# One decode step on one core: D-vectors as rows in four column tiles, FFN columns at stride 3, a row store, and score sums in two halves

## The chip, the cores and the metric

The kernel runs on one core of a Trainium2 chip. The metric is the device time of one execution in microseconds (us), so lower is better. A time called "median" is that of the runs of one kernel in one set of rounds. The "span" of a profile goes from the first to the last instruction and is 1.7 to 2.2 us shorter than the device time of the same execution.

TensorE is written PE (PEld is its weight load), VectorE is DVE, ScalarE is ACT, and SP is the engine that issues most DMAs. LN2 is the second LayerNorm, and `aT` is gelu(gate) times up, the input of down. The "granted clock" is TensorE's, as a share of full speed; the "DMA share" is the mean busy share of the core's 16 DMA engines.

## The reference, cut to what matters

```python
x = A_x                                          # [2, 1, 640], bf16
mod = (silu(c) @ w_mod).reshape(2, 6, 1, -1)     # w_mod [640, 3840]
sa, ca, ga, sb, cb, gb = ...                     # six 640-vectors per row
h = layernorm(x) * (1 + ca) + sa
# attention: 32 heads of 192, the last 1024 of 4096 cached keys
q = h @ wq                                       # wq [640, 6144]
o = softmax(q k^T / sqrt(192)) v
x = x + ga * (o @ wo)                            # wo [6144, 640]
h = layernorm(x) * (1 + cb) + sb
x = x + gb * ((gelu(h @ w_gate) * (h @ w_up)) @ w_down)   # F = 1536
```

There are two batch rows and one query position each. Nearly all the work is reading weights and cache: 76.9 MB.

## The kernel before

Loads are issued in a fixed order from SP: w_mod, then a ring of eight 1.5 MB slots (five of wq, 16 K and 16 V tiles, six of wo), then w_gate, w_up and w_down in three pieces. A slot is loaded again as soon as its reader is done. So the last bytes to arrive are those of w_down, and everything that must be done after their arrival lies bare.

A D-vector (640 numbers per batch row) is kept "transposed": element p*5+j is on partition p. A product that makes such a vector uses the weights as the stationary operand, read with a stride, and two moving columns:

```python
for tl in range(WOT):                     # wo; w_mod and w_down alike
    for j in range(KT):                   # KT = 5: stride 5
        e.matmul(ps[:, BK_M, 2*j:2*j+2], lhsT=wv[:, tl, :, j], rhs=oT[:, t, :], ...)
# gate and up: FC = 12 tiles, so stride 12
lhsT=wv[:, k, :].rearrange("p (m f) -> p m f", f=FC)[:, :, fc]
# ... (cut)
# the score sums of a tile: three pieces of 16, 8 and 8 columns
CHUNKS = [(0, J // 2), (J // 2, J // 4), (3 * J // 4, J // 4)]
# ... (cut)
WD_SPLIT = [(0, 6), (6, 4), (10, 2)]      # w_down's three loads, of 12
# ... (cut)
S.dma("sp", k_dma(out.rearrange("b o (p j) -> p (b o) j", j=KT), finb[:, :, :]), ...)
```

The store at the end therefore writes five neighbouring numbers (10 bytes) per partition and batch row: 256 pieces.

Of the kernel before, what the change touches and what calls it, by code (L numbers as in the profile page):

```python
# [5 lines left out]
ALU = mybir.AluOpType  # L6
# [97 lines left out]
def bass_adaLN_cond__sliding_block_cached__geglu_ffn__decode_kernel(  # L104
# [21 lines left out]
    NQ = H * Dh  # L126
    HQ = 4
# [5 lines left out]
    DD = Dh // NT  # L133
    FC = F // P
    assert B == 2 and D == KT * P and J * PH == W and NQD * HQ == H and NT * P == NQ
    assert DD * NT == Dh and DD * H == P and FC * P == F and J % 8 == 0
    SCALE = float(Dh) ** -0.5
    EPS = 1e-5
    NEG = 1e30
    GC = 512 // J  # L140
    NCH = Dh // GC
    assert GC * NCH == Dh
# [5 lines left out]
    assert SLOT == NQ  # L148
    WOT = 8
    NWO = NT // WOT  # L150
    assert NWO * WOT == NT and WOT * D <= SLOT
    CHUNKS = [(0, J // 2), (J // 2, J // 4), (3 * J // 4, J // 4)]
    WD_SPLIT = [(0, 6), (6, 4), (10, 2)]
    assert FC == 12
    X0 = HQ * DD * (NQD - 1) + DD - 1
    ZW = X0 + DD * (HQ - 1) + P
    QW = 2 * Dh
    NQB = NQ // (HQ * QW)

    es = ExitStack()  # L160
    with es:
# [10 lines left out]
        prod = sb("prod", [P, 2, J, Dh], BF16)  # L172
        qbc = sb("qbc", [P, B, NQD, Dh], BF16)
        qrow = sb("qrow", [P, NQ // HQ], BF16)
# [4 lines left out]
        mask4 = sb("mask4", [P, HQ], F32)  # L179
        mneg = sb("mneg", [P, HQ], BF16)  # L180
        maskc = sb("maskc", [P, P], F32)
        selq = sb("selq", [P, B, P], BF16)
        ztmp = sb("ztmp", [P, 4, 2, HQ], BF16)
        zsel = sb("zsel", [P, 2, ZW], BF16)
        rows = sb("rows", [2 * B, D], BF16)
        scT = sb("scT", [P, KT, B], BF16)
        X2 = sb("X2", [P, 2, KT, B], F32)
        st4 = sb("st4", [P, 4], F32)
        mv = sb("mv", [P, 8], F32)
        rstd = sb("rstd", [P, 2], F32)  # L190
        modT = sb("modT", [P, 6, KT, B], F32)
        opc = sb("opc", [P, 2, KT, B], F32)
        lnt = sb("lnt", [P, 2, KT, B], F32)
# [13 lines left out]
        fin = sb("fin", [P, KT, B], F32)  # L207
        finb = sb("finb", [P, B, KT], BF16)
        ps = es.enter_context(nc.psum_tensor("ps", [P, 8, 512], F32))

        BK_S = (0, 1)
        BK_Q = (2, 3)
# [3 lines left out]
        BK_M = 7  # L216

# [3 lines left out]
        sem_x = S.sem("d_x")  # L221
# [6 lines left out]
        sem_out = S.sem("d_out")  # L228
# [4 lines left out]
        items = [("wq", k) for k in range(KT)] + [("k", 0)]  # L233
        for g in range(1, NG):
            items += [("k", g), ("v", g - 1)]
        items += [("v", NG - 1)] + [("wo", i) for i in range(NWO)]
# [6 lines left out]
        def ring_src(it):  # L243
            kind, i = it
            if kind == "wq":
                return A_wq.rearrange("(p k) n -> p k n", k=KT)[:, i, :], NQ
            if kind == "wo":
                return A_wo.rearrange("(p t) n -> p t n", t=NT)[:, i * WOT:(i + 1) * WOT, :].rearrange("p t n -> p (t n)"), WOT * D
            quad, b = group(i)
            src = A_k_cache if kind == "k" else A_v_cache  # L250
            return src[b, quad * HQ:(quad + 1) * HQ, K0:Sk, :].rearrange("h (p j) d -> p h (j d)", p=PH), SLOT

        def declare_ring(consumed=()):
            ring_state["done"].update(consumed)
            while ring_state["next"] < len(items):
# [8 lines left out]
        S.dma("act", k_dma(rows[0:B, :], c[:, :]), sem_c, writes=["rows"], name="ld_c")  # L264
        S.dma("act", k_dma(rows[B:2 * B, :], A_x.rearrange("b o d -> (b o) d")), sem_x, writes=["rows_x"], name="ld_x")
        wm_dma = S.dma("sp", k_dma(wm_v.rearrange("p k n -> p (k n)"), w_mod.rearrange("(p k) n -> p (k n)", k=KT)), sem_wm,
                       writes=["wm"], name="ld_wm")
        declare_ring()

# [6 lines left out]
             reads=["ident_f"], writes=["ident_b"], name="ident_b")  # L276
        for b in range(B):
# [6 lines left out]
                                                in_=ones_b[:, 0:1].unsqueeze(2).broadcast_to([P, 4, 2 * HQ]),  # L284
                                                pattern=[[-32, 4], [-1, 2 * HQ]],
# [4 lines left out]
        S.op("dve", lambda e: e.memset(ps[:, 0:4, 0:QW], 0.0), writes=[bank(k) for k in range(4)], name="init_Q")  # L290
        S.op("dve", lambda e: e.memset(ps[:, BK_O, 0:ON], 0.0), writes=[bank(BK_O)], name="init_O")
        S.op("dve", lambda e: e.tensor_reduce(out=mask4[:, :], in_=ident_f[:, :].rearrange("p (x h) -> p h x", h=HQ), axis=AX.X, op=ALU.add),
             reads=["ident_f"], writes=["mask4"], name="mask4")

        cx_ps = ps[:, BK_M, 256:256 + 2 * KT].bitcast(BF16).rearrange("p (j r) -> p j r", j=KT)

        def cx_T(e):
            last = None
            for j in range(KT):
                last = e.transpose(cx_ps[:, j, :], rows[:, :].rearrange("r (p j) -> r p j", j=KT)[:, :, j], ident_b[0:2 * B, 0:2 * B])  # L300
            return last
        S.op("pe", cx_T, reads=["rows", "rows_x", "ident_b"], writes=[bank(BK_M)], name="cxT")
        S.op("act", lambda e: e.activation(out=scT[:, :, :], in_=cx_ps[:, :, 0:B], func=ACTF.Silu),
             reads=[bank(BK_M)], writes=["scT"], name="silu")
        S.op("dve", lambda e: e.tensor_copy(out=X2[:, 0, :, :], in_=cx_ps[:, :, B:2 * B]),
             reads=[bank(BK_M)], writes=[("X2", 0)], name="x_f32")

        def ln_norm(tag):
            S.op("dve", lambda e: e.tensor_tensor(out=X2[:, 1, :, :], in0=X2[:, 0, :, :], in1=X2[:, 0, :, :], op=ALU.mult),
                 reads=[("X2", 0)], writes=[("X2", 1)], name=tag + "_sq")  # L310
            S.op("pe", lambda e: e.matmul(ps[:, BK_M, 448:448 + 4 * KT], lhsT=ones_f[:, :],
                                          rhs=X2[:, :, :, :].rearrange("p q j b -> p (q j b)"), start=True, stop=True),
                 reads=[("X2", 0), ("X2", 1), "ones_f"], writes=[bank(BK_M)], name=tag + "_stat")
            S.op("dve", lambda e: e.tensor_reduce(out=st4[:, :].rearrange("p (q b) -> p q b", q=2),
                                                  in_=ps[:, BK_M, 448:448 + 4 * KT].rearrange("p (q j b) -> p q b j", q=2, j=KT),
                                                  axis=AX.X, op=ALU.add),
                 reads=[bank(BK_M)], writes=["st4"], name=tag + "_sum")
            S.op("dve", lambda e: e.tensor_scalar(out=mv[:, 0:4], in0=st4[:, :], scalar1=1.0 / D, scalar2=None, op0=ALU.mult),
                 reads=["st4"], writes=[("mv", 0)], name=tag + "_mean")
            S.op("dve", lambda e: e.tensor_tensor(out=mv[:, 4:6], in0=mv[:, 0:2], in1=mv[:, 0:2], op=ALU.mult),  # L320
                 reads=[("mv", 0)], writes=[("mv", 1)], name=tag + "_msq")
            S.op("dve", lambda e: e.scalar_tensor_tensor(out=mv[:, 6:8], in0=mv[:, 2:4], scalar=EPS, in1=mv[:, 4:6],
                                                         op0=ALU.add, op1=ALU.subtract),
                 reads=[("mv", 0), ("mv", 1)], writes=[("mv", 2)], name=tag + "_var")
            S.op("act", lambda e: e.activation(out=st4[:, 0:2], in_=mv[:, 6:8], func=ACTF.Sqrt),
                 reads=[("mv", 2)], writes=["st4"], name=tag + "_sqrt")
            S.op("dve", lambda e: e.reciprocal(out=rstd[:, :], in_=st4[:, 0:2]),
                 reads=["st4"], writes=["rstd"], name=tag + "_rstd")
            for b in range(B):
                S.op("dve", (lambda b: lambda e: e.tensor_scalar(out=lnt[:, 0, :, b], in0=X2[:, 0, :, b],  # L330
                                                                  scalar1=mv[:, b:b + 1], scalar2=rstd[:, b:b + 1],
                                                                  op0=ALU.subtract, op1=ALU.mult))(b),
                     reads=[("X2", 0), ("mv", 0), "rstd"], writes=[("lnt", 0, b)], name=tag + "_xn%d" % b)

        def ln_mod(tag, opc_idx, s_idx, dst_bf):
            S.op("dve", lambda e: e.tensor_tensor(out=lnt[:, 1, :, :], in0=lnt[:, 0, :, :], in1=opc[:, opc_idx, :, :], op=ALU.mult),
                 reads=[("lnt", 0, 0), ("lnt", 0, 1), ("opc", opc_idx)], writes=[("lnt", 1)], name=tag + "_mulc")
            S.op("dve", lambda e: e.tensor_tensor(out=dst_bf[:, :, :], in0=lnt[:, 1, :, :], in1=modT[:, s_idx, :, :], op=ALU.add),  # L338
                 reads=[("lnt", 1), ("modT", s_idx)], writes=[tag + "_out"], name=tag + "_out")

        ln_norm("ln1")
        S.op("dve", lambda e: e.tensor_scalar(out=mneg[:, :], in0=mask4[:, :], scalar1=-1.0, scalar2=NEG, op0=ALU.add, op1=ALU.mult),
             reads=["mask4"], writes=["mneg"], name="mneg")
# [5 lines left out]
             reads=["ztmp", "zsel"], writes=["zsel"], name="zsel")  # L349

        mod_pe = []

        def mod_part(part, i0, i1):
            def f(e):
                last = None
# [43 lines left out]
        def q_unit():  # L399
            if qstate["n"] >= len(qunits):  # L400
                return
# [268 lines left out]
```

## Time and profile before

| what | value | where it is read |
|---|---|---|
| device time | 195.04 us, median of 3 | times |
| span | 193.1 us | page |
| share of DMA in the chain that ended last | 81% | page, part 4 |
| DMA rate in the loop | 424 to 425 GB/s, share 1.01 | windows |
| PE and DVE in 30 us of the loop | 22 and 20 us busy | windows |
| last piece of w_down has landed | 186.4 us | semaphore events |
| end of down | 188.45 us | timeline |
| store issued, landed | 188.90, 192.7 us | timeline, DMA issues |

Three lines of the page of the kernel before: the busy share of the DMA engines in 40 slices of the span (9 is 90% or more), the bytes they moved, and the queue that fetches instructions (packets, MB, share).

```profile
DMA  7999999999999999999999999999999999999910
GB/s 255 438 392 428 426 428 425 423 428 428 428 421 428 426 425 419 431 417 433 416 433 420 426 422 422 428 422 428 421 425 428 420 415 431 414 435 423 378 71 1
q8 instruction: 13, 0.21, 0.4%
```

The DMA engines are full from the second slice to the 38th. The Trainium skill, "DMA: Bandwidth & Descriptors", Specifications, gives 435 GB/s as the fabric ceiling; the 424 GB/s of the loop agree with it. No reordering of compute inside the loop can speed that up.

The windows view of the kernel before: start and end of the window, its length, then busy time (and instructions) of PE, PEld, DVE, ACT and POOL, then granted PE clock, DMA share and GB/s.

```profile
60.00:90.00 30.00, 22.89 (x279) 17.25 (x278) 20.05 (x35) 5.40 (x15) 0.00 (x0) 0.92 1.01 424
90.00:120.00 30.00, 21.60 (x275) 16.02 (x272) 19.93 (x33) 3.93 (x12) 0.00 (x0) 0.94 1.01 425
182.00:184.00 2.00, 2.00 (x37) 2.00 (x35) 0.00 (x0) 0.00 (x0) 0.00 (x0) 0.50 0.73 297
184.00:186.00 2.00, 1.65 (x30) 1.57 (x29) 0.18 (x1) 0.00 (x0) 0.00 (x0) 0.50 0.29 112
186.00:188.00 2.00, 2.00 (x53) 2.00 (x54) 0.00 (x0) 0.00 (x0) 0.00 (x0) 0.50 0.00 0
```

In the loop, PE and DVE have a quarter to a third of their time free. At the end, the DMA share falls over four microseconds, from 0.73 to nothing: the 16 engines do not finish together.

The end of the timeline of the kernel before: start, duration (both us), engine, line, operation, output and inputs, and in brackets the idle time of the engine just before and what ended it.

```profile
181.80 3.75 PE L587 MATMUL ps<-h2T,r 128*128 128x2 bf16 x60 [0.27 <-DMA r<-in_B_w_up_dram]
185.65 0.18 DVE L598 TENSOR_TENSOR aT<-ps,gl 128x24 bf16<-128x24 f32 x1 [7.94 <-PE ps L587]
185.89 2.56 PE L606 MATMUL ps<-aT,r 128*128 128x2 bf16 x60 [0.35 <-DVE aT L598]
188.49 0.17 DVE L612 TENSOR_TENSOR fin<-ps,modT 128x10 f32<-128x10 f32 x1 [2.65 <-PE ps L606]
188.69 0.18 DVE L615 TENSOR_TENSOR finb<-fin,X 128x10 bf16<-128x10 f32 x1
188.90 0.40 SPq L231 DMA_DIRECT2D out_dram<-finb  x1
```

The up-projection (L587) starts as w_up lands and needs 62.5 ns per matmul. Down (L606) starts when `aT` is ready, not when its weights land. So when the last w_down piece lands at 186.4 us, the kernel is about 2 us behind.

### The profile page before, as it was taken

Reading aid. Unit: us, or ns where it says so; the run is one execution under the profiler, and the core shown is the slowest. Engines: PE = TensorE matmul, PEld = TensorE weight load, DVE = VectorE, ACT = ScalarE, POOL = GpSimd, SP = SyncE. Lnnn points to the kernel's source line nnn. Section 1 sums busy time; section 2 is a strip of 40 time slices with the busy share of each in tenths; the row PEclk is TensorE's granted clock in tenths of the full one; section 3 lists DMA queues with packets and bytes.
Section 4 is the critical chain, followed back from the end, with each engine's and each line's share of the span. In section 5 each row is a group of like instructions: output and inputs, shape, how many; then the busy total and the mean of one; then the engine's idle time right before and its main releaser. Section 6 shows DMA issues by size and latency. Waiting matters only on the chain.

```text
span 193.1 us, 3891 instructions
## 1 busy us (share of the span) xinstructions
PE 124.5 (64%) x1723; PEld 95.2 (49%) x1723; DVE 86.4 (45%) x164; ACT 28.3 (15%) x70; POOL 2.6 (1%) x12
## 2 busy tenths in 40 slices
PE   0108932479768777597597586596595858563990
PEld 0108600158446556475375355384374538463990
DVE  3221000396847747658649549559556600004000
ACT  2300000303211312201101101201111231003000
POOL 5000000000000000000000000000000000000000
PEclk9999999999996999969879999969969975555555
DMA  7999999999999999999999999999999999999910
GB/s 255 438 392 428 426 428 425 423 428 428 428 421 428 426 425 419 431 417 433 416 433 420 426 422 422 428 422 428 421 425 428 420 415 431 414 435 423 378 71 1
DMA packets 7353, 77.13 MB, mean 399 GB/s; under 512 B 1060, under 2 KB 1064, under 8 KB 1448
## 3 DMA queue, kind: packets, MB, share of 16 engines
q1 hardware_dynamic: 7328, 76.88, 94.7%
q8 instruction: 13, 0.21, 0.4%
q14 instruction: 4, 0.03, 0.0%
q10 hardware_dynamic: 8, 0.01, 0.0%
HBM read 76.88 MB, written 0.00 MB: 398 GB/s over the span
## 4 chain that ended last, share of the span: by engine, by line
DMA 81%; DVE 6%; PE 6%; issue 3%; SPq 1%; DVEq 0%
DMA ring<-in_A_k_cache_dram 53%; DMA r<-in_B_w_up_dram 15%; DMA ring<-in_A_wq_dram 13%; DVE prod L419 4%; PE ps L587 2%; PE ps L432 1%; PE ps L606 1%; SPq L231 1%; DVE S_sb L439 1%; PE ps L382 1%; DVE nmx L449 0%; DVE M L442 0%; DVE rden L493 0%; DVE aT L598 0%; DVE finb L615 0%
## 5 line engine op out<-in xcount | busy, mean ns | idle before, releaser
L432 PE MATMUL ps<-prod,ident_b 128*128 128x128 bf16 (+1 forms) x576 | 59.1, 261 | 28.1 <-DVE prod L419 28.0
L419 DVE TENSOR_TENSOR prod<-ring,qbc 128x1536 bf16<-128x1536 bf16 (+1 forms) x48 | 58.1, 1214 | 26.4 <-DMA ring<-in_A_k_cache_dram 26.4
L432 PEld LDWEIGHTS ps<-prod,ident_b 128*128 128x128 bf16 x576 | 45.3, 108 | 42.4 <-DVE prod L419 37.8
L495 ACT ACTIVATE On<-ps,rden 128x384 bf16<-128x384 f32 x16 | 9.3, 580 | 42.8 <-DVE rden L493 39.5
L556 PE MATMUL ps<-oT,ring 128*128 128x2 bf16 x240 | 10.4, 179 | 5.3 <-DMA ring<-in_A_wo_dram 4.9
L484 PE MATMUL ps<-ring,E_sb 128*8 128x384 bf16 x256 | 13.4, 330 | 0.0
L556 PEld LDWEIGHTS ps<-oT,ring 128*128 128x128 bf16 x240 | 10.0, 131 | 5.8 <-DMA ring<-in_A_wo_dram 5.2
L467 ACT ACTIVATE E_sb<-Sb_sb 128x128 bf16<-128x128 f32 x16 | 4.9, 309 | 47.1 <-DVE Sb_sb L464 47.1
L382 PE MATMUL ps<-ring,hT 128*2 128x384 bf16 x80 | 7.1, 517 | 7.2 <-DMA ring<-in_A_wq_dram 7.2
L439 DVE TENSOR_REDUCE S_sb<-ps 128x32 f32<-128x512 f32 x16 | 10.8, 673 | 1.3 <-PE ps L432 1.3
L359 PE MATMUL ps<-scT,r 128*128 128x2 bf16 x150 | 6.3, 179 | 6.4 <-DMA r<-in_w_mod_dram 6.2
L359 PEld LDWEIGHTS ps<-scT,r 128*128 128x128 bf16 x150 | 6.2, 131 | 6.6 <-issue 6.3
L587 PE MATMUL ps<-h2T,r 128*128 128x2 bf16 x120 | 7.5, 199 | 2.5 <-DVE h2T L338 2.2
L587 PEld LDWEIGHTS ps<-h2T,r 128*128 128x128 bf16 x120 | 7.3, 164 | 2.7 <-DVE h2T L338 2.3
L574 DVE TENSOR_TENSOR lnt<-ps,modT 128x10 f32<-128x10 f32 x1 | 0.2, 169 | 17.9 <-PE ps L556 17.9
L473 PE MATMUL ps<-denp,maskc 128*128 128x1 f32 x32 | 6.1, 260 | 3.0 <-ACT E_sb L467 2.6
L382 PEld LDWEIGHTS ps<-ring,hT 128*2 128x2 bf16 x80 | 2.1, 108 | 11.5 <-DMA ring<-in_A_wq_dram 9.5
L464 DVE TENSOR_TENSOR Sb_sb<-S_sb,ps 128x128 f32<-128x128 f32 x16 | 4.6, 288 | 6.4 <-PE ps L459 6.4
L473 PEld LDWEIGHTS ps<-denp,maskc 128*128 128x128 f32 x32 | 4.8, 188 | 5.3 <-ACT E_sb L467 5.2
L393 DVE CAST qrow<-ps 128x384 bf16<-128x384 f32 x2 | 1.0, 553 | 13.8 <-PE ps L382 13.8
L458 PE MATMUL ps<-nmx,ones_f 1*128 1x4 f32 x32 | 6.5, 271 | 0.4 <-DVE nmx L449 0.4
L449 DVE TENSOR_REDUCE nmx<-ps 1x4 f32<-1x128 f32 x16 | 4.5, 278 | 4.7 <-PE ps L444 4.7
(64 smaller groups left out, 75.9 us busy)
## 6 DMA issues: line engine op xcount, KB each, us to landing
ring<-in_A_k_cache_dram SPq DMA_DIRECT2D x16, 1536.0 KB, 24.9
ring<-in_A_v_cache_dram SPq DMA_DIRECT2D x16, 1536.0 KB, 26.0
ring<-in_A_wq_dram SPq DMA_DIRECT2D x5, 1536.0 KB, 24.7
ring<-in_A_wo_dram SPq DMA_DIRECT2D x6, 1280.0 KB, 24.0
r<-in_w_mod_dram SPq DMA_DIRECT2D x1, 4800.0 KB, 14.2
r<-in_B_w_gate_dram SPq DMA_DIRECT2D x1, 1920.0 KB, 25.6
r<-in_B_w_up_dram SPq DMA_DIRECT2D x1, 1920.0 KB, 29.7
r<-in_B_w_down_dram SPq DMA_DIRECT2D x1, 960.0 KB, 31.6
```

Source lines behind the costliest of these rows:

```text
L359: last = e.matmul(ps[:, BK_M, (i * KT + j) * 2:(i * KT + j) * 2 + 2], lhsT=wm_v[:, k, i * D:(i + 1) * D].rearrange("p (m j) -> p m j", j=K ...
L382: last = e.matmul(ps[32 * i:32 * i + B, n, 0:QW].rearrange("p (q d) -> p q d", d=Dh), lhsT=hT[:, k, :], rhs=wv[:, 2 * n:2 * n + 2, i, :], ...
L419: S.op("dve", lambda e: e.tensor_tensor(out=prod[:, z, j0:j0 + nj, :], in0=ring[:, sl, j0 * Dh:(j0 + nj) * Dh].rearrange("p (j d) -> p j d ...
L432: last = e.matmul(o_ap, lhsT=ident_b[:, :], rhs=prod[:, z, j0:j0 + nj, t * GC:(t + 1) * GC], start=(ci == 0 and t == 0), stop=(t == NCH - ...
L439: S.op("dve", lambda e: e.tensor_reduce(out=S_sb[:, z, :], in_=ps[:, BK_S[z], :].rearrange("p (j c) -> p j c", c=GC), axis=AX.X, op=ALU.ad ...
L458: e.matmul(o_ap, lhsT=ones_f[0:1, :], rhs=nmx[:, z, :], start=True, stop=False)
L467: S.op("act", lambda e: e.activation(out=E_sb[:, z, :, :], in_=Sb_sb[:, z, :, :], func=ACTF.Exp, scale=SCALE, accum_out=denp[:, z:z + 1]), ...
L473: S.op("pe", lambda e: e.matmul(ps[:, BK_T, P + 8:P + 9], lhsT=maskc[:, :], rhs=denp[:, z:z + 1], start=True, stop=True), reads=[("denp", ...
L484: last = e.matmul(ps[32 * i:32 * i + 2 * HQ, BK_O, 0:ON], lhsT=E_sb[:, z, 2 * jp:2 * jp + 2, :].rearrange("p j h -> p (j h)"), rhs=ring[:, ...
L495: S.op("act", lambda e: e.activation(out=On[:, z, :], in_=ps[:, BK_O, 0:ON], func=ACTF.Identity, scale=rden[:, z:z + 1]), reads=[bank(BK_O ...
L556: last = e.matmul(ps[:, BK_M, 2 * j:2 * j + 2], lhsT=wv[:, tl, :, j], rhs=oT[:, t, :], start=(t == 0 and j == 0), stop=(t == NT - 1), skip ...
L587: last = e.matmul(ps[:, bk, fc * 2:fc * 2 + 2], lhsT=wv[:, k, :].rearrange("p (m f) -> p m f", f=FC)[:, :, fc], rhs=h2T[:, k, :], start=(k ...
```

## The change

The intent is to take work out of the tail. D-vectors become rows: partition 32*i+b holds elements 160*i to 160*i+159 of batch row b. A product that makes one has the two activations as stationary operand and 160 weight columns as moving operand, in four column tiles of the array. The FFN's columns are dealt to 12 tiles in blocks of three neighbours, so that gate and up read weights with stride 3, and the rows of w_down are loaded to match. The store writes rows of 320 bytes. In the loop, the score sums of a tile come in two halves, and the eight broadcasts of q are all made before the loop, with a memset that waits for them.

```diff
# down (wo and w_mod alike)
-                    for j in range(KT):
-                        last = e.matmul(ps[:, 2, 2 * j:2 * j + 2], lhsT=wd_v[:, fc, :].rearrange("p (m j) -> p m j", j=KT)[:, :, j],
-                                        rhs=aT[:, fc, :], ...)
+                    wv = wd_v[:, fc, :].rearrange("p (i n) -> p i n", i=NR)
+                    for i in range(NR):
+                        last = e.matmul(ps[32 * i:32 * i + B, BK_OT, CY:CY + DR], lhsT=aT[:, fc, :], rhs=wv[:, i, :],
+                                        start=(fc == 0), stop=(fc == FC - 1), tile_position=(0, 32 * i))
# gate and up
-                                        lhsT=wv[:, k, :].rearrange("p (m f) -> p m f", f=FC)[:, :, fc],
+                                        lhsT=wv[:, k, a * P * FR:(a + 1) * P * FR].rearrange("p (m r) -> p m r", r=FR)[:, :, r],
# w_down's loads: three pieces, the last of 3 (before 2) of 12
-        wd_src = B_w_down.rearrange("(p f) n -> p f n", f=FC)
+        wd_src = B_w_down.rearrange("(a p r) n -> p a (r n)", a=FA, r=FR)
# store
-        S.dma("sp", k_dma(out.rearrange("b o (p j) -> p (b o) j", j=KT), finb[:, :, :]), sem_out, ...)
+        for b in range(B):
+            S.dma(("sp", "act")[b], k_dma(out[b, 0, :].rearrange("(i n) -> i n", i=NR), finb[b:P:32, :]), sem_out[b], ...)
# LN2's row is transposed back for gate and up: 20 small matmuls and a copy
+                for j in range(KT):
+                    for i in range(NR):
+                        last = e.matmul(ps[32 * i:32 * i + 32, BK_M, CT + 2 * j:CT + 2 * j + 2], lhsT=hv[:, :, j], rhs=selrow[:, i, :], ...)
# loop: halves of 16 columns instead of 16, 8, 8
-                d_mul(g, 2)
-                declare_ring([("k", g)])
-                p_reduce(g, 2)
+                p_reduce(g, 1)
# ... (LayerNorm on rows, masks, x loaded as rows, wo in pieces of 9 tiles: cut)
```

## The prediction

> **What bounds the kernel.** The loads. The chain of waits is 81% DMA; from 18 us on the windows view shows a DMA share of 1.01 at 424 to 430 GB/s, up to about 182 us. (The Trainium skill, "DMA: Bandwidth & Descriptors", Specifications, gives 435 GB/s as the fabric ceiling; the trace agrees.) In the middle DVE works about 20 us of 30 and PE 22 of 30, so neither limits. 76.9 MB are read before and after, so the stream is the floor, and only what lies after its end can shrink.
>
> **The tail before (timeline, semaphore landings).** The last w_down piece lands about 186.4 us into the span. The up-projection starts when w_up lands (181.75) and needs 3.75 us, aT follows at 185.65, the 60 down matmuls run 185.89 to 188.45, two DVE operations end at 188.87, the store is issued at 188.90 and lands 3.8 us later. The span is 193.1 us, the device time 195.04.
>
> **What the change does there.**
> - Down: 60 matmuls with strided weights (43 ns each) become 48 with 160 moving columns in four column tiles. PV, of the same kind with 384 columns, ran at 52 ns each; I estimate 25 to 35 ns. Only 12 (0.3 to 0.4 us, plus about 0.3 us latency) follow the last piece.
> - FFN: gate and up took 62.5 ns per matmul at stride 12, wo and down 43 ns at stride 5. "SBUF — State Buffer" says that accesses that cross to a new 16-byte line pay; the two strides agree. At stride 3 I expect about 43 ns: 2.6 instead of 3.75 us for each of gate and up. So up ends about 184.4, aT 184.7: no longer late; the last w_down piece becomes the limit.
> - Chain after wo: wo's remainder falls from 1.76 to about 0.5 us, but LN2 gains a Square, 160-wide DVE operations (0.25 to 0.3 us instead of 0.17) and a 20-matmul transpose with copy, about 1 us. A wash: gate starts about 177.5 (177.77 before), bounded by w_gate's landing at 177.2.
> - Store: 256 pieces of 10 bytes become two DMAs of four 320-byte rows. Before, the first of 16 engines landed after 2.55 us and the last after 3.8; I estimate 2.2 to 2.6 us.
>
> New tail: 186.4 + 0.7 (down) + 0.6 (DVE) + 2.4 (store) + 0.4 = about 190.5, so about 2.7 us less.
>
> **What it moves without effect.** mod (150 matmuls, 6.3 us) falls to 40, perhaps 3 us. All eight q broadcasts come before the loop, and a 1.34 us memset waits for them, so the first multiplication starts about 4 us later. The ring holds some 25 us of queued loads (issue to landing 24.9 us), and DVE needs about 5.2 us of each 7.4 us group, so it catches up. Score sums in halves: 24 matmuls of 152 ns instead of 12 of 152 and 24 of 78; the same.
> Upside: 13 instruction fetches of 16 KB (about 1 us each on one DMA engine) become 10 or 11; the last landings spread over 3.4 us between engines, so the stream may end up to 1 us earlier.
>
> **Predicted: 192.2 us**, 8 in 10 between 190.9 and 193.6. Chances: faster by over 2% 0.15, within 2% 0.84, slower 0.01.
>
> **What would show it.** Right: w_down's last landing near 186.4, up's matmuls near 43 ns, down ending within 0.8 us of that landing, store landing below 2.7 us, DMA share still 1.01 in the loop. Wrong: gaps in DMA in the loop; stride 3 as slow as stride 12; gate starting after 178.5; a store as slow as before; a stream end that moves by over 1 us, since the slowest DMA engine sets it.

## The result, and the profile after

The changed kernel takes 192.07 us (median of 4, 191.83 to 192.23) against 194.91 us of the kernel before in the same rounds. The ratio is 0.9854, with a 95% interval of 0.9837 to 0.9871. By the 2% measure the two are the same; the difference of 2.8 us is real all the same, since the interval excludes 1.

The same three lines of the page, of the kernel after:

```profile
DMA  7999999999999999999999999999999999999960
GB/s 259 388 416 441 423 427 428 418 436 426 418 429 426 421 427 425 421 428 424 423 426 431 418 423 434 419 421 431 428 416 434 420 423 424 426 421 432 399 252 8
q8 instruction: 11, 0.18, 0.4%
```

The stream is as full as before. Its 39th slice reads 6 instead of 1 because the slices are shorter (190.5/40 us), so that this one starts at 181.0 us instead of 183.5.

The windows view of the kernel after, in the loop and at the end:

```profile
60.00:90.00 30.00, 19.29 (x228) 14.40 (x226) 20.16 (x30) 4.36 (x13) 0.00 (x0) 1.00 1.01 424
184.00:186.00 2.00, 1.32 (x36) 0.88 (x36) 0.00 (x0) 0.00 (x0) 0.00 (x0) 0.50 0.25 95
186.00:188.00 2.00, 0.79 (x20) 0.23 (x12) 0.53 (x2) 0.00 (x0) 0.00 (x0) 0.50 0.01 4
```

PE is 3.6 us less busy in these 30 us of the loop, and the DMA rate there is the same 424 GB/s. After the stream, PE is busy 0.79 us of the two microseconds where it was busy throughout.

The end of the timeline of the kernel after:

```profile
181.79 1.81 PE L605 MATMUL ps<-h2T,r 128*128 128x2 bf16 x60 [1.73 <-DMA r<-in_B_w_up_dram]
183.71 0.18 DVE L616 TENSOR_TENSOR aT<-ps,gl 128x24 bf16<-128x24 f32 x1 [5.53 <-PE ps L605]
184.57 1.65 PE L625 MATMUL ps<-r,aT 128*2 128x160 bf16 x36 [0.97 <-DMA r<-in_B_w_down_dram]
186.81 0.57 PE L625 MATMUL ps<-r,aT 128*2 128x160 bf16 x12 [0.60 <-DMA r<-in_B_w_down_dram]
187.44 0.32 DVE L630 TENSOR_TENSOR fin<-ps,modR 128x160 f32<-128x160 f32 x1 [3.55 <-PE ps L625]
187.80 0.32 DVE L632 TENSOR_TENSOR finb<-fin,X 128x160 bf16<-128x160 f32 x1
188.15 0.66 SPq L246 DMA_DIRECT2D out_dram<-finb  x1
```

Up starts at the same moment, when w_up lands, but takes 1.81 us instead of 3.75. Down now waits for its weights, twice (the two brackets naming w_down). Only 12 matmuls follow the last landing. The store's last semaphore event comes at 190.07 us, 1.92 us after the issue, instead of 3.82 us.

The whole difference can be laid out from these lines and the landings:

| | before | after | difference |
|---|---|---|---|
| last w_down landing | 186.41 | 186.77 | +0.36 |
| from there to the end of down | 2.04 | 0.61 | -1.43 |
| to the store's issue (two DVE operations) | 0.45 | 0.77 | +0.32 |
| store, issue to landing | 3.82 | 1.92 | -1.90 |
| to the end of the span | 0.41 | 0.43 | +0.02 |
| span | 193.13 | 190.5 | -2.63 |

One line of this table was not expected: the last landing came 0.36 us later, although the same bytes were loaded. These are single profiles: a_store_pieces and a_stride12 below, with the same loads and as many fetches, landed it at 186.37 and 186.23 us. So what can be said is that it did not come earlier. Looked at event by event, each load has 16 semaphore events, which the Trainium skill ("DMA: Bandwidth & Descriptors", "Why a DMA increments its semaphore by 16 and not by 1") explains as one per DMA engine; the trace shows 16 for each of these loads. The first engine landed its share of the last w_down piece at 183.02 us before and at 183.13 us after; the slowest came 3.38 and 3.64 us after that. The experiments on fetches below take this up.

### The profile page after: what moved, and what is told of

Read it like the earlier page. It is cut to its first block, busy times and chain, and to the rows that moved or that the text cites. A ratio compares the mean times of both kernels' runs of the same rounds, so it can differ in the third digit from the quotient of the medians.

```text
span 190.5 us, 3243 instructions
## 1 busy us (share of the span) xinstructions
PE 109.4 (57%) x1401; PEld 74.3 (39%) x1401; DVE 88.7 (47%) x147; ACT 29.2 (15%) x74; POOL 3.0 (2%) x14
## 4 chain that ended last, share of the span: by engine, by line
DMA 71%; DVE 13%; SPq 5%; PE 4%; issue 3%; ACT 2%
DMA ring<-in_A_k_cache_dram 39%; DMA ring<-in_A_wq_dram 16%; DMA r<-in_B_w_down_dram 16%; DVE prod L441 8%; SPq L246 5%; PE ps L454 3%; DVE S_sb L461 2%; ACT qbc L433 2%; PE ps L416 1%; DVE ps L436 1%; DVE M L464 1%; PE ps L480 0%; DVE rden L516 0%; PE ps L625 0%; DVE Sb_sb L486 0%
## 5 line engine op out<-in xcount | busy, mean ns | idle before, releaser
L441 DVE TENSOR_TENSOR prod<-ring,qbc 128x3072 bf16<-128x3072 bf16 x32 | 55.9, 1752 | 21.7 <-DMA ring<-in_A_k_cache_dram 21.7
L454 PE MATMUL ps<-prod,ident_b 128*128 128x256 bf16 x384 | 53.4, 296 | 21.0 <-DVE prod L441 21.0
L454 PEld LDWEIGHTS ps<-prod,ident_b 128*128 128x128 bf16 x384 | 38.2, 105 | 33.1 <-DVE prod L441 25.4
L480 PEld LDWEIGHTS ps<-nmx,ones_f 1*128 1x128 f32 x32 | 5.1, 198 | 20.3 <-DVE nmx L471 20.3
L575 PE MATMUL ps<-ring,oT 128*2 128x160 bf16 x192 | 7.2, 333 | 8.3 <-DMA ring<-in_A_wo_dram 7.8
L575 PEld LDWEIGHTS ps<-ring,oT 128*2 128x2 bf16 x192 | 5.4, 115 | 9.9 <-DMA ring<-in_A_wo_dram 9.3
L530 PEld LDWEIGHTS ps<-On,zsel 128*128 128x128 bf16 x128 | 6.1, 110 | 1.2 <-ACT On L518 1.2
L530 PE MATMUL ps<-On,zsel 128*128 128x48 bf16 x128 | 6.0, 187 | 0.8 <-ACT On L518 0.8
L506 PEld LDWEIGHTS ps<-ring,E_sb 128*8 128x8 bf16 x256 | 4.9, 86 | 3.0 <-issue 0.5
L396 PE MATMUL ps<-r,scT 128*2 128x480 bf16 x40 | 4.3, 596 | 2.1 <-DMA r<-in_w_mod_dram 2.1
```

Source lines behind the costliest of these rows:

```text
L441: S.op("dve", lambda e: e.tensor_tensor(out=prod[:, 2 * (g % 2) + ci, :, :], in0=ring[:, sl, ci * JC * Dh:(ci + 1) * JC * Dh].rearrange("p ...
L454: last = e.matmul(o_ap, lhsT=ident_b[:, :], rhs=prod[:, pz, :, t * GC:(t + 1) * GC], start=(ci == 0 and t == 0), stop=(t == NCH - 1), skip ...
L480: e.matmul(o_ap, lhsT=ones_f[0:1, :], rhs=nmx[:, z, :], start=True, stop=False)
L506: last = e.matmul(ps[32 * i:32 * i + 2 * HQ, BK_O, 0:ON], lhsT=E_sb[:, z, 2 * jp:2 * jp + 2, :].rearrange("p j h -> p (j h)"), rhs=ring[:, ...
L530: last = e.matmul(ps[:, BK_OT, b * NT:(b + 1) * NT], lhsT=zsel[:, jj, x:x + P], rhs=On[:, z, jj * Dh + dd * NT:jj * Dh + (dd + 1) * NT], s ...
L575: last = e.matmul(ps[32 * i:32 * i + B, BK_M, 0:DR], lhsT=oT[:, t, :], rhs=wv[:, tl, i, :], start=(t == 0), stop=(t == NT - 1), tile_posit ...
```

## The experiments

The theory: the loads are a floor, the gain is the tail's, and it has two parts, the store's shape (about 1.9 us) and the lateness of down behind its last weights (about 1.4 us). Rivals: the relieved loop and the smaller number of PE instructions give the gain; the store's shape matters little; or all time saved in up counts. All seven kernels ran for five rounds, so each is compared with the kernel before on the same chip (194.92 us for the first four, 195.03 us for the last three).

### The store in pieces again

```diff
-        for b in range(B):
-            S.dma(("sp", "act")[b], k_dma(out[b, 0, :].rearrange("(i n) -> i n", i=NR), finb[b:P:32, :]), sem_out[b], ...)
+        S.dma("sp", k_dma(out.rearrange("b o (p j) -> p (b o) j", j=KT), finb[:, 0:B * KT].rearrange("p (b j) -> p b j", b=B)), sem_out[0], ...)
```

> The changed kernel, with its store put back to one DMA of 256 pieces of 10 bytes from 128 partitions (the values stored are then the wrong ones, on purpose; everything up to the store is unchanged). Theory (the row store is the largest term of the gain): the store lands about 3.8 us after its issue, as before, instead of 1.9 us, so the time rises by 1.9 us to about 194.0. Rival (a store is mostly fixed cost, and its shape matters little): within 0.4 us of 192.1.

It took 194.0 us (median of two groups of three, 193.44 to 193.64 and 194.36 to 194.43; the profile is of the lower one), ratio to before 0.9955 (0.9938 to 0.9973). The result is wrong, as intended. In the profile the store was issued at 187.75 us. Two lines show its landing: the DMA issues of this run (KB, us from issue to landing), and what SP waited for (us in total, times, longest).

```profile
out_dram<-finb SPq DMA_DIRECT2D x1, 2.5 KB, 3.7
SPq L636 <- DMA out_dram<-finb: 3.3, 1, 3.3
```

The same wait in the kernel after, which has the row store:

```profile
SPq L640 <- DMA out_dram<-finb: 1.0, 1, 1.0
```

So the shape of a 2.5 KB store is worth about 1.9 us by the medians (1.4 to 2.4 by the single runs; 1.77 from issue to landing in the two profiles), two thirds of the gain, and the rival that a store is fixed cost falls. The run changes the size of the pieces and their number together with the use of two queues; which of these counts most was not separated.

### FFN columns back at stride 12

```diff
-        wd_src = B_w_down.rearrange("(a p r) n -> p a (r n)", a=FA, r=FR)
+        wd_src = B_w_down.rearrange("(p a r) n -> p a (r n)", a=FA, r=FR)
-                                        lhsT=wv[:, k, a * P * FR:(a + 1) * P * FR].rearrange("p (m r) -> p m r", r=FR)[:, :, r],
+                                        lhsT=wv[:, k, :].rearrange("p (m f) -> p m f", f=FC)[:, :, fc],
```

> The changed kernel, with the FFN columns back at stride 12 (w_down's rows permuted to match, results right). Both theories: gate and up back to about 62 ns per matmul, 3.75 us each. Theory (the last w_down piece, landing at about 186.8 us, hides most of up): up ends at 185.5, aT at 185.75, the 36 first down matmuls are about 1 us late, the end only 0.4 to 0.6 us: about 192.6. Rival (every nanosecond of up is on the critical path, since it waits for w_up): plus 1.9 us, about 194.0.

It took 192.41 us, ratio 0.988 (0.9867 to 0.9892), against 192.07 us of the changed kernel in the rounds of the result. The timeline of this run:

```profile
178.08 7.28 PE L605 MATMUL ps<-h2T,r 128*128 128x2 bf16 x120 [0.28 <-DVE h2T L376]
185.46 0.18 DVE L616 TENSOR_TENSOR aT<-ps,gl 128x24 bf16<-128x24 f32 x1 [7.44 <-PE ps L605]
185.70 1.77 PE L625 MATMUL ps<-r,aT 128*2 128x160 bf16 x48 [0.34 <-DVE aT L616]
```

Gate and up together are 3.66 us slower, and `aT` is 1.75 us later; the kernel lost 0.34 us by the medians, which are of different rounds (about 0.5 us by the two ratios). The rest was slack: down's weights were not there anyway. In this run the last piece landed at 186.23 us, and down ended 1.24 us after it. (In the profile of the kernel after it landed 0.54 us later, so the ends of down in the two profiles, 187.47 and 187.38 us, must not be subtracted.)

### Stride 3 alone, in the kernel before

```diff
-    WD_SPLIT = [(0, 6), (6, 4), (10, 2)]
+    WD_SPLIT = [(0, 6), (6, 3), (9, 3)]
-        wd_src = B_w_down.rearrange("(p f) n -> p f n", f=FC)
+        wd_src = B_w_down.rearrange("(a p r) n -> p a (r n)", a=4, r=3)
-                                        lhsT=wv[:, k, :].rearrange("p (m f) -> p m f", f=FC)[:, :, fc],
+                                        lhsT=wv[:, k, (fc // 3) * P * 3:(fc // 3 + 1) * P * 3].rearrange("p (m r) -> p m r", r=3)[:, :, fc % 3],
# and the loads of w_down by blocks of three rows, as in the change
```

> The kernel before, with the FFN columns at stride 3 alone (w_down's rows permuted to match, its last piece now three of twelve rows, results right). Theory: gate and up at 30 ns per matmul; up ends at about 183.6 instead of 185.6, and down is then bound by the last w_down piece (186.4): 15 matmuls of 43 ns after it end at 187.2 instead of 188.45: minus 1.0 to 1.3 us, about 193.8. Rival (additive): minus 1.9 us, about 193.0.

It took 193.85 us, ratio 0.9952 (0.9937 to 0.9967), so 1.07 us less by the medians. The timeline of this run:

```profile
181.72 1.76 PE L587 MATMUL ps<-h2T,r 128*128 128x2 bf16 x60 [2.15 <-DMA r<-in_B_w_up_dram]
184.17 1.93 PE L606 MATMUL ps<-aT,r 128*128 128x2 bf16 x45 [0.69 <-DMA r<-in_B_w_down_dram]
186.43 0.76 PE L606 MATMUL ps<-aT,r 128*128 128x2 bf16 x15 [0.32 <-DMA r<-in_B_w_down_dram]
```

Up is 2.0 us faster, but from there on down waits for weights. The last piece landed at 186.38 us and down ended 0.81 us later. Four numbers now tell how far down's end lies behind the last landing: 2.04 us with neither part, 1.24 with column-tiled down alone, 0.81 with stride 3 alone, 0.61 with both. The two savings (0.80 and 1.23) do not add up to the joint 1.43, because each hides part of the other behind the same landing. (In the two kernels with late `aT` the lag also depends on where the landing falls, 186.41 and 186.23 us, so the sizes are good to some tenths.)

### The loop alone, in the kernel before

```diff
-    CHUNKS = [(0, J // 2), (J // 2, J // 4), (3 * J // 4, J // 4)]
+    CHUNKS = [(0, J // 2), (J // 2, J // 2)]
-        q_unit()
-        q_unit()
+        for _ in qunits:
+            q_unit()
# and the third piece and the q_unit of each loop pass taken out
```

> The kernel before, with the attention loop of the change alone (score sums in two halves per tile, all q broadcasts before the loop). Theory (the loads are the floor and the ring hides the loop): no change, within 0.3 us of 194.9; TensorE has 384 instructions fewer, so 12 instead of 13 instruction fetches, and the last landings still spread over 3.4 us. Rival (the relieved loop or fewer TensorE instructions give the gain): minus 1 us or more.

It took 195.18 us, ratio 1.0018 (1.0006 to 1.003). There were 12 instruction fetches, the last landings spread over 3.45 us, and the last one came at 186.56 us. The loop part of the change gains nothing, and the rival falls. This run has the halves and the early broadcasts; the memset that follows the broadcasts is not in it.

### Instruction fetches: three kernels

The spread between DMA engines remained. The landings show it growing in steps: one of 16 engines falls back by about 1.5 us shortly after each 16 KB packet of the instruction queue, and does not catch up again; the windows leave it no free time to do so (DMA share 1.01). In the kernel before, for instance, a fetch started at 139.3 us, and an engine that had landed its share of one load about 1.9 us after the first engine landed the next load 3.41 us after it. The Trainium skill, "Runtime: NRT & Kernel Launch", Instruction fetch mechanics, says that an engine's instructions are refilled in blocks of 16 KiB, which are 256 instructions. The counts agree to within one packet: 3446 PE instructions (1723 matmuls, each with a weight load), 13.5 blocks of 256, gave 13 packets, and 2802, 10.9 blocks, gave 11. The theory added to the first: fetches go round eight DMA engines, and what counts is whether one of them is hit twice (or three times) while it has loads left.

First, fewer PE instructions, by 512-wide score sums:

```diff
+            if ci == 0:
+                return
-                    last = e.matmul(o_ap, lhsT=ident_b[:, :], rhs=prod[:, pz, :, t * GC:(t + 1) * GC], ...)
+                    last = e.matmul(o_ap, lhsT=ident_b[:, :], rhs=prod[:, pz:pz + 2, :, t * GC:(t + 1) * GC], ...)
```

> The changed kernel, with each tile's score sums as 12 matmuls of 512 columns after both halves, instead of 24 of 256: 384 TensorE instructions fewer of 2802 (each matmul counts with its weight load). Theory (each 16 KB instruction fetch delays one DMA engine by about 1.5 us; fetches go round some eight engines, so the ninth gives one engine a second delay, and that engine lands the last w_down piece): 9 fetches instead of 11, but the ninth still comes at about 182 us, while the engines have w_down left, so the last landing stays near 186.3 us and the time within 0.5 us of 192.0. Rivals: the spread between engines has nothing to do with fetches (no change, and the same for the next run); or the gain goes with the number of TensorE instructions (about a proportional 1 us).

Second, the same with the selection of two neighbouring groups joined:

```diff
+            if b == 0:
+                return
-                        last = e.matmul(ps[:, BK_OT, b * NT:(b + 1) * NT], lhsT=zsel[:, jj, x:x + P],
-                                        rhs=On[:, z, jj * Dh + dd * NT:jj * Dh + (dd + 1) * NT], ...)
+                        last = e.matmul(ps[:, BK_OT, 0:B * NT].rearrange("p (b t) -> p b t", b=B), lhsT=zsel[:, jj, x:x + P],
+                                        rhs=On[:, :, jj * Dh + dd * NT:jj * Dh + (dd + 1) * NT], ...)
```

> As a_red512, and the selection matmuls of two neighbouring groups joined (64 matmuls of 96 columns instead of 128 of 48): 128 TensorE instructions fewer again, 2290 in all. Theory: the ninth fetch comes only during or after the last down matmuls, so no engine is delayed twice while it has loads left; the landings of the last w_down piece spread over about 2.1 us instead of 3.3 to 3.6, it lands at about 185.2 us, and the time falls by 1.2 to 1.6 us to about 190.6. Rival (the spread is not of fetches): within 0.3 us of a_red512.

Third, more PE instructions in the loop, where PE has room:

```diff
                 p_pv(g - 1)
                 declare_ring([("v", g - 1)])
+                S.op("pe", lambda e: [e.matmul(ps[0:2, 2, 0:2], lhsT=ident_b[:, 0:2], rhs=ident_b[:, 0:2], start=True, stop=True)
+                                      for _ in range(56)][-1], reads=["ident_b"], writes=[bank(2)], ...)
```

> The changed kernel with 56 matmuls of 2 columns added after each of the 16 PV steps (1792 TensorE instructions, 4594 in all; their result is not used). TensorE has room in the loop (about 21 us busy of 30). Theory of the fetches: 17 of them, the 17th at about 178 us gives one engine a third delay, the landings of the last w_down piece spread over 4.5 to 5 us, the time rises by 1.0 to 1.5 us to about 193.3, with the loop's DMA share still 1.01. Rival (the loop hides it, the spread is not of fetches): within 0.3 us of 192.1.

| kernel | PE instructions | fetches | last landing | time | ratio to before (interval) |
|---|---|---|---|---|---|
| before | 3446 | 13 | 186.41 | 194.91 | |
| after | 2802 | 11 | 186.77 | 192.07 | 0.9854 (0.9837 to 0.9871) |
| a_red512 | 2418 | 9 | 186.46 | 191.98 | 0.9845 (0.9832 to 0.9859) |
| a_few_pe | 2290 | 9 | 185.31 | 190.77 | 0.9782 (0.9769 to 0.9796) |
| a_pad56 | 4594 | 18 | 187.75 | 193.29 | 0.9917 (0.9904 to 0.993) |

The times of the first two rows are from the rounds of the result. This is when each engine landed its share of the last w_down piece, in us after the first one, sorted. It is worked out from the semaphore events of each trace; the engines themselves are not named there.

```
before    0.00 0.05 0.05 0.14 0.50 0.72 0.80 1.51 1.64 1.86 1.88 1.91 2.97 3.13 3.25 3.38
after     0.00 0.06 0.10 0.28 0.73 0.76 0.85 1.50 1.52 1.57 1.67 1.89 1.95 2.10 3.30 3.64
a_red512  0.00 0.08 0.12 0.16 0.63 0.67 0.92 0.98 1.37 1.51 1.53 1.59 1.78 1.80 1.95 3.27
a_few_pe  0.00 0.06 0.10 0.21 0.78 0.86 0.89 1.09 1.49 1.50 1.66 1.66 1.69 1.95 1.99 2.16
a_pad56   0.00 0.08 0.11 0.23 0.66 0.87 0.96 1.24 2.92 2.97 3.02 3.09 3.12 3.31 3.42 4.59
```

In all five the first engine landed between 183.02 and 183.19 us, so what moves the last landing is the laggards alone. The last three rows read like a tally of the fetches on each engine. With a_pad56, 17 fetches came in time (an 18th at 187.0 us was too late to matter): eight engines have none, seven have two, one has three. With a_red512, nine came in time: seven engines have one, one has two. With a_few_pe, the ninth came at 184.6 us, when eight engines had landed their share and the other eight had at most 0.8 us to go: eight engines have one, and none has two. Its time fell by 1.21 us against a_red512 in the same rounds, for only 128 instructions fewer; a_red512 itself had removed 384 and gained nothing measurable. A smooth cost per instruction cannot do that. Of the runs above, a_store_pieces and a_stride12 (ten fetches in time: two engines with two, six with one) and b_loop_halves (eleven: three and five) fit the tally too.

The first two rows, and b_stride3, have one engine more near 1.5 us than the count would give. The landings, followed load by load, point to what delayed it: a second instruction queue, q14, whose packets have 8 KB. These are its lines on the page of the kernel before and, below it, of the kernel after:

```profile
q14 instruction: 4, 0.03, 0.0%
q14 instruction: 3, 0.02, 0.0%
```

Whose instructions it fetches is not named. After its packets, too, one engine falls back, by about 0.6 to 1.0 us: in the kernel after, the packet at 75.6 us took an engine from 0.48 to 1.47 us behind the first; in the kernel before, the one at 160.3 us took one from 0.99 to 1.99 us, and in b_stride3 the one at 162.7 us took one from 1.02 to 1.94 us. No run changed these packets, so this rests on their times alone. In the last three rows such engines stay at 1.24 us or less, among those counted as having none.

That it is not the loop, which the padding also fills, is shown by the windows view of a_pad56:

```profile
60.00:90.00 30.00, 25.87 (x491) 21.62 (x487) 20.14 (x30) 4.19 (x13) 0.00 (x0) 1.00 1.01 423
120.00:152.00 32.00, 26.66 (x451) 21.37 (x449) 20.69 (x30) 3.93 (x12) 0.00 (x0) 0.93 1.01 423
```

The DMA share stays 1.01. And at the end, the last down matmuls of a_few_pe and, below them, of a_pad56:

```profile
185.35 0.57 PE L628 MATMUL ps<-r,aT 128*2 128x160 bf16 x12 [0.60 <-DMA r<-in_B_w_down_dram]
```

```profile
187.79 0.57 PE L627 MATMUL ps<-r,aT 128*2 128x160 bf16 x12 [0.59 <-DMA r<-in_B_w_down_dram]
```

It is the same work, started by the same landing, 2.4 us apart; the times of the two kernels are 2.5 us apart. a_few_pe gives right results and beats both kernels: 190.77 us, 2.2% below the kernel before.

## Why the prediction was right

The forecast was 192.2 us, the measurement 192.07 us; the forecast span of about 190.5 us was met as well. Point by point:

- **The loads are the floor.** Right: the same rate and share in the loop after the change, and the loop's part alone gave nothing (ratio 1.0018).
- **Stride 3 makes up faster, and then the last w_down piece is the limit.** The mechanism was right: down's brackets now name w_down, and two runs show that only part of up's saving counts. The size was off, harmlessly: 30 ns per matmul instead of 43, as the slack behind w_down's landing absorbs it.
- **Down costs little after the last landing.** Right: 0.61 us against 0.7 forecast. A column-tiled matmul took 37 ns (1.77 us for 48) instead of 25 to 35. The two DVE operations after it, with their gaps, took 0.77 us instead of 0.6.
- **The store.** Right in kind, but the saving was undersized: the store landed after 1.92 us instead of 2.2 to 2.6.
- **The chain after wo is a wash.** Gate started at 178.24 us instead of 177.5. The two timeline lines of the kernel after below show why (the input of the square root was ready at 175.70 us, 0.74 us before it started): the table for the square root was loaded only after the statistics matmul, and the square root waited for the load. The gate still ended 1.73 us before w_up landed, so this cost nothing.

```profile
175.14 1.28 ACT L354 ACT_TABLE_LOAD   x1 [0.78 <-PE ps L345]
176.44 0.20 ACT L354 ACTIVATE st<-nvar 128x1 f32<-128x1 f32 x1
```

- **The loop starts later and catches up.** Right: the first multiplication began at 41.97 us instead of 38.01, and the stream did not notice. (mod fell to 4.3 us of busy time, not 3.)
- **Fewer fetches may end the stream up to 1 us earlier.** This did not come: with 11 fetches the stream ended at 186.2 to 186.8 us (three profiles), with 13 at 186.4. The step that was mis-sized took the number of fetches for the cost. The runs showed that it is the largest number on one engine, two in both kernels. With at most one per engine, the gain was there (a_few_pe).

The forecast total came out so close partly by luck, because errors cancelled: in the profiled execution the store was about 0.5 us better than assumed, the stream's end 0.36 us and the DVE operations 0.17 us worse.

## What to carry to other kernels

In a kernel bound by its loads, list what still has to happen after the last byte lands, and shorten only that; a saving earlier in the chain counts only up to the next landing, and two savings before the same landing do not add. Look at the landings of the last load engine by engine: if they spread, look for what else uses some of the DMA engines; here it was the fetching of a long unrolled PE program, where 128 instructions, by which the ninth fetch came 2.9 us later, were worth 1.2 us. Try to store the result in few long pieces even if it is tiny; here that was worth about 1.9 us.

## What the Trainium skill lacked or had wrong

- "Runtime: NRT & Kernel Launch", Instruction fetch mechanics, calls the cost of crossing a 16 KiB boundary mostly hidden. With full DMA engines it is not: each fetch set one engine back by about 1.5 us (about 1.9 to 3.41 us in the example), and a second one on the same engine cost 1.2 us of the whole time (191.98 against 190.77 us).
- No page that I read says over how many DMA engines the fetches of one engine's instructions go. The landings of a_pad56 (3.0, 4.6 and at most 1.24 us behind the first) read as 17 fetches with two each on seven engines and three on an eighth, and none on the other eight.
- "SBUF — State Buffer", the note on cachelines, says both that two accesses per 16-byte line are needed for full bandwidth and that bf16 can stride by 8 elements for free. For PE weight loads the first fits better and the second fails: a 128x128 bf16 weight load with its 2-column matmul took 30 ns at stride 3, 43 ns at stride 5 and 62.5 ns at stride 12, all at a granted clock of 0.50.
- "DMA: Bandwidth & Descriptors" gives a minimum of 512 bytes for full rate, and no figure for a tiny store by its shape. Here 2.5 KB landed in 3.7 to 4.0 us (four kernels) as 256 pieces of 10 bytes, and in 1.9 to 2.0 us (five kernels) as eight of 320 bytes over two queues.
